# An mLSTM cell and an FP32 feed-forward on one core: products nobody reads from the first microsecond, other buffers for the second chunk's values, and a new order of the front

## The chip, the cores and the metric

The kernel runs on one core of a Trainium2 chip. The core has TensorE (PE, matrix products, with a weight load PEld that overlaps them), VectorE (DVE), ScalarE (ACT), GpSimd (POOL) and SyncE (SP), whose queue issues the DMAs here. The metric is device microseconds of one execution; a profiled execution is looked at beside it.

## The reference

Two stages follow each other. The first is an mLSTM cell over q, k, v of shape (4 batches, 8 heads, 768 steps, 40), with an input, a forget and an output gate:

```python
for t in range(S):
    m_new = np.maximum(f_gate[:, :, t] + m, i_gate[:, :, t])
    f_stab = np.exp(f_gate[:, :, t] + m - m_new)
    i_stab = np.exp(i_gate[:, :, t] - m_new)
    m = m_new
    C = f_stab * C + i_stab * (v_t outer k_t)
    n = f_stab * n + i_stab * k_t
    h_tilde = C @ q_t
    denom = np.maximum(np.abs(n @ q_t), 1.0)
    y[:, :, t] = sigmoid(o_gate[:, :, t]) * h_tilde / denom
```

The loop's bodies are shortened here to what they compute per batch and head. The second stage takes y as 3072 rows of 320, multiplies by w_in (320 x 2048), applies the exact GELU and multiplies by w_out (2048 x 320). The weights lie in DRAM as pairs of 32-bit words, the high and low halves of an FP64 number: the kernel turns them into FP32 itself.

## The kernel before

**Chunks and batches.** The 768 steps are cut into six chunks of 128 (`NCH`), and each chunk has four batches, so a step of the cell is named by a chunk c and a batch b. For chunk 0 the state is zero. `Cell` holds the steps of one chunk. Each step is one letter: `m` mask, `w` weights (the matrix of decays, exponentials on ACT), `g` output gate (a sigmoid on ACT), `t` turn (PE transposes of k and q, copied by ACT), `s` scores (PE, then multiplied into the weights by DVE), `c` carry (PE products into the state and of the state), `v` values (PE), `y` finish (DVE: gate and denominator), `x` turn_y (PE transposes of y, copied by ACT into the feed-forward's input), `r` split_x. Lower case is chunk 0, capitals are chunk 1; the digit behind a letter is the batch.

**Feed-forward.** The rows of chunk 0 go through plain FP32 products: `A` and `U` are up steps (`up_step`, PE and a GELU on ACT; `A` for batches 0 and 1, `U` for 2 and 3), `F` is one of sixteen down rows (`first_down_steps`). Later chunks use products that are split into parts or summed differently (`up`, `down_steps`); the diff does not touch those.

**Weights.** They come in 26 pieces: ten of w_in, sixteen of w_out. `P` fetches a piece; `K` is `conv_one` of the next piece (three DVE operations, two ACT operations), `J` is `conv_two` (two DVE operations), which then fetches the piece four further on. `Z` is `split_weight`, which makes two parts of a piece of w_in for the next chunk's rows.

**The order is written by hand.** `FRONT` is a string of such words, and `play` (near the end of the file) calls the function of each word in turn. Every engine keeps its instructions in that program order, and so does SP's queue of DMAs. An engine waits at an instruction until what it reads is there and what it overwrites is free; all that stands behind on that engine waits too. One exception is in `play`: up steps that were asked for are issued when the next other word comes, or when two are together (`U U`).

**Words of the front that are not of the cell.** `L` loads q and k of a step, `O` v and the output gate. `E` (`second_gates`) and `N` (`later_gates`) compute the gates of chunk 1 and of chunks 2 to 5 with DVE scans, turn them on PE and store the running maximum in DRAM (`M_d`); `B` (`load_M`) loads it back, broadcast. `D` and `Q` (`decays_turned`) turn decay factors: PE transposes, DVE copies, one PE product with `last`. `H` (`products_begin`) opens the pool of later tiles.

**Unread products.** `I` (`keep_clock`) leaves a count in `idle`; the next step that opens a PSUM bank first does that many products of `ident` with itself into it (`unread`), which the real products then overwrite. A later `I` replaces an earlier count that was not used:

```python
def unread(bank):
    for _ in range(idle[0]):
        nc.tensor.matmul(bank, ident, ident, start=True, stop=True, skip_group_check=True)
    idle[0] = 0
```

In the order before, 1 such product stands ahead of w0, 3 ahead of v1, 5 ahead of c1, 2 ahead of s2 and 7 ahead of c2.

**Buffers.** PSUM has the pools `ps_tr` (tag "tr"), `ps_h` (tag "h") and `ps_mm` (tags "a" and "b"), with two buffers for each tag. `carry` and `values` of chunks 0 and 1 take turns in `ps_h`; in chunk 0 the bank of `values` is read by `finish`. From chunk 1 on, `carry` writes what the state gives to a tile `far` (L489), to which `values` adds its part (L527), and which `finish` reads. `far` lies in a pool of two (tag "hs"). The output rows leave through `o_sb`, two buffers of 128 x 2 x 320.

Of the kernel before, what the change touches and what calls it, by code (L numbers as in the profile page):

```python
# [9 lines left out]
F32 = mybir.dt.float32  # L10
# [6 lines left out]
P = 128  # L17
# [8 lines left out]


FRONT = """
    O0 L0 I1 I1 g0 E L1 P0 O2 P1 w0 t0 N D K w1 L2 P2 Q P3 s0 O1 t1 w2 L3 c0 J K v0 K s1 y0 w3 t2 I3 g1 v1 O3 I2 I3
    I5 J c1 B5 I2 K y1 I4 I2 s2 x0 O4 L4 t3 J x1 B4 s3 v2 I7 g3 L5 g2 c2 c3 y2 v3 x2 O5 L6 K J G0 A y3 x3 J H M0 M1  # L30
    K K J T0 W0 O6 M2 O7 A J W1 S0 C0 K J T1 L7 U U K K V0 T2 A M3 J J G1 S1 K W2 W3 K C1 A S2 V1 G2 J Y0 J K
    C2 T3 J K Y1 U U J S3 V2 C3 K J K K J J F K F F F J K J X0 K K J F R0 F F J F K G3 Y2 F J K V3 J K F K X1 J
    J R1 F F F F K X2 B8 J R2 F Y3 Z Z X3 R3 B9 B10 F"""
DOWN = """
    M0 Z M1 W0 F L3 F W1 Z Z F S0 Z S1 K2 C0 M2 Z C1 G0 G1 G2 G3 V0 Z V1 W2 Z M3 F Q2 K3 Q3 Y0 D3 F F W3 F Z S2 S3
    C2 C3 V2 V3 F N F Y1 X0 R0 Y2 F F Y3 X1 R1 F X2 R2 F X3 R3 F"""
# [3 lines left out]
def kernel(  # L40
# [16 lines left out]
    nc = tc.nc  # L57

    B, H, S, D = q.shape
    L = P  # L60
    NCH = S // L
    NP = H // 2
    D1 = D + 1
    DP = 64
    BH = B * H
    DM = H * D
# [15 lines left out]
    two = ctx.enter_context(tc.tile_pool(name="two", bufs=2))  # L82
    outp = ctx.enter_context(tc.tile_pool(name="outp", bufs=2))
    dram = ctx.enter_context(tc.tile_pool(name="dram", bufs=1, space=bass.MemoryType.DRAM))
    ps_tr = ctx.enter_context(tc.tile_pool(name="ps_tr", bufs=2, space=bass.MemoryType.PSUM))
    ps_h = ctx.enter_context(tc.tile_pool(name="ps_h", bufs=2, space=bass.MemoryType.PSUM))
# [9 lines left out]
    w_out = const.tile([P, NF, DM], F32, name="w_out")  # L96
# [32 lines left out]
    def load(n, first=0, end=4):  # L129

        if n >= NCH * B:
            return
        c, b = divmod(n, B)
        for src, dst in ((q, qb), (k, kb), (v, vb), (o_gate, None))[first:end]:
            nc.sync.dma_start(out=dst[turn_of(n)][:, :, 0:D] if dst else out_of(n),
                              in_=src[b, :, c * L:(c + 1) * L, :].rearrange("h p d -> p h d"))
# [13 lines left out]
    def turn_of(n):  # L150

        return n % NLD if n < 2 * B else (n - 2 * B) % NQ
# [38 lines left out]
    for j in range(3):  # L191
        m = slice(BH * j, BH * (j + 1))
        nc.scalar.copy(out=row[m], in_=ident[m, m])
    nc.vector.memset(e_hi, 1151.0 * I23)
    nc.vector.memset(e_lo, 255.0 * I23)

# [5 lines left out]
    def gates_turned(*parts):  # L202

        for src, dst in parts:
            n = dst.shape[1]
            pg = ps_tr.tile([P, n, BH], F32, name="pg", tag="tr")
            for c in range(n):
                nc.tensor.transpose(pg[:, c, :], src[:, c, :], ident[0:BH, 0:BH])
            nc.vector.tensor_copy(out=dst, in_=pg)
# [24 lines left out]
    def decays_turned(e0, e1, g0, g1):  # L234
        e, g = slice(e0, e1), slice(g0, g1)
        gates_turned((ew[:, e], ewT[:, e]), (gg[:, g], gT[:, g]))
        pd = ps_tr.tile([P, g1 - g0, BH], F32, name="pd", tag="tr")
        nc.tensor.matmul(pd.rearrange("p c n -> p (c n)"), last, gT[:, g].rearrange("p c n -> p (c n)"),
                         start=True, stop=True)
        nc.vector.tensor_copy(out=dec[:, g], in_=pd)  # L240
# [4 lines left out]
    for j in range(3):  # L245
        part = M_parts[BH * j:BH * (j + 1)]
        nc.vector.tensor_copy(out=part, in_=left)
        if j < 2:
            nc.vector.tensor_tensor(out=M_left[:, j], in0=left, in1=part, op=OP.subtract)
            left = M_left[:, j]  # L250
    gates_turned((a[:, 0:1], aT[:, 0:1]))

    def second_gates():
        gates_of(1, 2)
        nc.sync.dma_start(out=M_d[0], in_=M[:, 1])
        gates_turned((a[:, 1:2], aT[:, 1:2]))
        decays_of(0, 2, 0, 1)
# [65 lines left out]
    def conv_two(i):  # L323

        if i < len(pieces):
            hi, p = bits.pop(i)[:, :, 1], pow2.pop(i)
            pu = p.bitcast(U32)
            nc.vector.scalar_tensor_tensor(out=pu, in0=hi, scalar=0x80000000, in1=pu,
                                           op0=OP.bitwise_and, op1=OP.bitwise_or)
            dst, s = pieces[i][1], sig.pop(i)  # L330
            nc.vector.scalar_tensor_tensor(out=dst, in0=s, scalar=2.0 ** -20, in1=p, op0=OP.mult, op1=OP.mult)
            fetch(i + NB)
# [10 lines left out]
# [5 lines that stand above are left out]
    def per_head(t, c, b):  # L348
        return t[:, c, b * H:(b + 1) * H].unsqueeze(2)

    class Cell:
# [112 lines left out]
        def carry(self, b):  # L464

            c, n = self.c, self.c * B + b
            qT = self.qT.pop(b)

            pf = ps_h.tile([P, H + NP, D1], F32, name="pf", tag="h")
            pc = pf[:, H:H + NP, :]  # L470
            unread(pf.rearrange("p h d -> p (h d)")[:, 0:P])
            if c == 0:
                self.weigh_values(b)
            if c + 1 < NCH:
                vw = self.vw.pop(b)
                for p in range(NP):
                    for hip in range(2):
                        nc.tensor.matmul(pc[halves[hip], p, :], kb[turn_of(n)][:, 2 * p + hip, :], vw[:, 2 * p + hip, :],  # L478
                                         start=True, stop=True)
            if c > 0:  # L480
                for p in range(NP):
                    for r in halves:
                        nc.tensor.matmul(pf[r, 2 * p:2 * p + 2, :].rearrange("p h d -> p (h d)"), qT[:, p, r],  # L483
                                         state[b][:, p, :], start=True, stop=True)
                if c > 1 and b == B - 1:
                    self.far[b] = qb[2].rearrange("p h d -> p (h d)")[:, 0:H * D1].rearrange("p (h d) -> p h d", d=D1)
                else:
                    self.far[b] = fars[0].tile([P, H, D1], F32, name="far", tag="hs", bufs=2)
                nc.vector.tensor_tensor(out=self.far[b], in0=pf[:, 0:H, :],  # L489
                                        in1=per_head(gT, c - 1, b).to_broadcast([P, H, D1]), op=OP.mult)  # L490
            if c + 1 < NCH:
                for hip in range(2):
                    r, m = halves[hip], slice(D1 * hip, D1 * hip + D1)
                    st = state[b][r, :, m]
                    if c == 0:
                        nc.scalar.copy(out=st, in_=pc[r])
                    else:
                        d = dec[r, c - 1, b * H:(b + 1) * H].rearrange("p (m two) -> p m two", two=2)[:, :, hip:hip + 1]
                        self.engine.tensor_tensor(out=st, in0=st, in1=d.to_broadcast([DP, NP, D1]), op=OP.mult)
                        nc.vector.tensor_tensor(out=st, in0=st, in1=pc[r], op=OP.add)  # L500

            self.read(b)
# [170 lines left out]
    def first_up_steps(h):  # L673

        def step(k):
            ups.append((len(ups) + len(tags_next) % 2, (2 * k, 2 * k + 2, HT * h, HT * h + HT)))
            if len(ups) == 2:
                first_up()

        return [lambda k=k: step(k) for k in range(HF // 2)]  # L680
# [78 lines left out]
    def first_down_steps(g):  # L759
        po = []  # L760

        def row(f):

            if f == 0:
                po.extend(ps_mm.tile([P, DM], F32, name="po", tag="ab"[b // 2]) for b in range(B))
            for b in range(B):
                nc.tensor.matmul(po[b], g.t[:, f, b * L:(b + 1) * L], w_out[:, f, :], start=(f == 0),  # L767
                                 stop=(f == NF - 1))
                if f == NF - 1:
                    if b % 2 == 0:  # L770
                        o_sb = outp.tile([P, 2, DM], F32, name="o_sb", tag="o_sb")
                    nc.scalar.copy(out=o_sb[:, b % 2, :], in_=po[b])
                    send(0, b, o_sb[:, b % 2, :])

        return [lambda f=f: row(f) for f in range(NF)]
# [75 lines left out]
    def in_turn(steps):  # L851
        todo = list(steps)
        return lambda: todo.pop(0)() if todo else None

    def cell_steps(c, letters, before=None):
# [6 lines left out]
    first_g = Hidden(False)  # L862
    n_pieces = range(len(pieces))
    steps = dict(P=fetch, L=lambda n: load(n, 0, 2), O=lambda n: load(n, 2, 4), B=load_M, E=second_gates, N=later_gates,
                 I=keep_clock, D=lambda: decays_turned(0, 2, 0, 1), Q=lambda: decays_turned(2, NCH - 1, 1, NCH - 1),
                 A=in_turn(first_up_steps(0)), U=in_turn(first_up_steps(1)), F=in_turn(first_down_steps(first_g)),
                 K=in_turn(lambda i=i: conv_one(i) for i in n_pieces), H=products_begin,
                 J=in_turn(lambda i=i: conv_two(i) for i in n_pieces), Z=split_weight)
# [42 lines left out]
```

## Time and profile before

The median of three runs is 490.48 us (489.78 to 490.59).

| Quantity | Value |
|---|---|
| The profiled execution's own time | 490.47 us |
| Its span, first to last instruction | 488.7 us |
| Mean granted PE clock | 0.990 |
| PE busy | 472.6 us, 97% of the span |
| DVE busy | 348.0 us, 71% |
| ACT busy | 222.8 us, 46% |
| POOL busy | 69.7 us, 14% |
| Start of the first up step (A) | 44.43 us |
| Start of the first down row (F) | 97.03 us |
| Start of chunk 1's up products | 135.14 us |

Each time in a profile is counted from the start of the span. "Busy" of PE is modelled from pipelined products, so two records can overlap. An FP32 product that is not a transpose shows as two records. A bracket behind an instruction tells how long its engine was idle before it and what ended the idle time.

### The profile page before, as it was taken

How to read it: one execution, taken by the hardware profiler on the slowest of the kernel's cores; microseconds unless marked ns; L12 is line 12 of the kernel's file. 1: busy time of each engine (PE TensorE's matmuls, PEld its weight loads, DVE VectorE, ACT ScalarE, POOL GpSimd, SP SyncE). 2: the span in 40 equal slices, each digit the busy share in tenths (PEclk: the TensorE clock that was granted, in tenths of full speed). 3: DMA queues.
4: the chain of work that ended last, by engine and by line, in shares of the span. 5: the costliest groups of instructions: out<-in, count | busy, mean ns of one | idle time of the engine just before them, and what ended most of it. 6: DMA issues, size and time to landing. Idle time of an engine off the chain costs nothing.

```text
span 488.7 us, 10729 instructions
## 1 busy us (share of the span) xinstructions
PE 472.6 (97%) x4184; PEld 412.8 (84%) x4184; DVE 348.0 (71%) x727; ACT 222.8 (46%) x477; POOL 69.7 (14%) x108
## 2 busy tenths in 40 slices
PE   3899999999999999999999999999999999999997
PEld 3687888877677899987899987899977899977996
DVE  7689787989889998857387757388857388724321
ACT  7595999845444662103762203762203762211300
POOL 3002120000010036200126200126100112000000
PEclk9599999999999999999999999999999999999999
DMA  6979954337561247831256921255931250100001
GB/s 117 236 187 197 239 128 96 107 107 170 102 166 15 27 75 123 166 94 19 31 90 104 200 62 16 34 89 102 190 73 20 32 91 2 36 20 1 1 0 55
DMA packets 164434, 44.24 MB, mean 91 GB/s; under 512 B 154176, under 2 KB 157408, under 8 KB 164384
## 3 DMA queue, kind: packets, MB, share of 16 engines
q1 hardware_dynamic: 164384, 43.56, 45.2%
q8 instruction: 33, 0.54, 0.5%
q14 instruction: 17, 0.14, 0.1%
HBM read 39.52 MB, written 4.01 MB: 89 GB/s over the span
## 4 chain that ended last, share of the span: by engine, by line
PE 88%; ACT 5%; DVE 4%; issue 1%; DMA 0%; SPq 0%; DVEq 0%; ACTq 0%
PE po L790 32%; PE pu L714 21%; PE po L767 7%; PE pu L725 6%; PE pu L659 5%; PE ps L459 4%; PE ph L519 4%; PE pf L483 2%; PE pf L478 2%; PE px L554 1%; PE pu L665 1%; ACT W L390 1%; ACT g L729 1%; PE pt L433 1%; ACT pow L316 1%
## 5 line engine op out<-in xcount | busy, mean ns | idle before, releaser
L790 PE MATMUL po<-w_out,g 128*128 128x160 f32 x640 | 91.2, 300 | 0.0
L729 ACT ACTIVATE g<-pu 128x512 f32<-128x512 f32 x80 | 40.8, 614 | 108.2 <-PE pu L725 108.0
L790 PEld LDWEIGHTS po<-w_out,g 128*128 128x128 f32 x640 | 87.8, 190 | 1.8 <-ACT g L729 1.8
L390 ACT ACTIVATE W<-W,aT 128x128 f32<-128x128 f32 x160 | 48.8, 389 | 3.2 <-POOL W L364 3.1
L790 PE MATMUL po<-w_sums,sums 128*128 128x160 f32 x320 | 47.2, 302 | 0.0
L790 PEld LDWEIGHTS po<-w_sums,sums 128*128 128x128 f32 x320 | 44.2, 190 | 0.4
L564 ACT ACTIVATE x_hi<-px 128x384 fp32r<-128x384 f32 x20 | 9.8, 490 | 73.0 <-PE px L554 73.0
L462 DVE TENSOR_TENSOR W<-ps,W 128x512 f32<-128x512 f32 x48 | 30.2, 684 | 17.4 <-ACT W L390 11.9
L714 PE MATMUL pu<-x_hi,w_in_hi 128*128 128x512 f32 x160 | 41.4, 400 | 0.0
L714 PE MATMUL pu<-x_lo,w_in_lo 128*128 128x512 f32 x160 | 40.6, 396 | 0.0
L364 POOL TENSOR_SCALAR_AFFINE_SELECT W<-W 128x1024 f32<-128x1024 f32 x20 | 23.1, 1162 | 102.8 <-DMA W<-M_d 102.5
L646 DVE TENSOR_TENSOR sums<-g 128x512 f32<-128x512 f32 x20 | 13.8, 690 | 33.3 <-ACT g L729 33.3
L714 PEld LDWEIGHTS pu<-x_hi,w_in_hi 128*128 128x128 f32 x160 | 29.4, 188 | 8.2 <-ACT g L729 1.9
L714 PEld LDWEIGHTS pu<-x_lo,w_in_lo 128*128 128x128 f32 x160 | 30.1, 188 | 7.2
L767 PE MATMUL po<-w_out,g 128*128 128x320 f32 x128 | 35.7, 434 | 0.0
L803 DVE TENSOR_TENSOR o_sb<-po,o_sb 128x320 f32<-128x320 f32 (+1 forms) x27 | 12.5, 465 | 28.7 <-PE po L790 24.9
L714 PE MATMUL pu<-x_all,w_in_mid 128*128 128x512 f32 x80 | 31.7, 396 | 0.1
L767 PEld LDWEIGHTS po<-w_out,g 128*128 128x128 f32 x128 | 23.8, 190 | 9.3
L714 PE MATMUL pu<-x_all,w_mid 128*128 128x512 f32 x80 | 31.7, 396 | 0.0
L618 DVE TENSOR_TENSOR w_in_mid<-w_in_hi,w_in_lo 128x512 fp32r<-128x512 f32 x20 | 14.7, 733 | 21.6 <-PE pu L714 21.6
L659 PE MATMUL pu<-first_x,w_in 128*128 128x256 f32 x128 | 28.8, 381 | 0.5 <-DVE W L462 0.5
L402 POOL MEMSET g<- 32x1024 f32 x8 | 7.6, 945 | 145.0 <-ACT W L390 144.8
(166 smaller groups left out, 882.3 us busy)
## 6 DMA issues: line engine op xcount, KB each, us to landing
W<-M_d SPq DMA_DIRECT2D x20, 512.0 KB, 5.0
bits<-in_moe_w_in_dram SPq DMA_DIRECT2D x20, 256.0 KB, 4.7
bits<-in_moe_w_out_dram SPq DMA_DIRECT2D x16, 320.0 KB, 3.2
ob<-in_o_gate_dram SPq DMA_DIRECT2D x24, 160.0 KB, 3.7
out_dram<-o_sb SPq DMA_DIRECT2D x24, 160.0 KB, 2.4
vb<-in_v_dram SPq DMA_DIRECT2D x22, 160.0 KB, 5.4
kb<-in_k_dram SPq DMA_DIRECT2D x22, 160.0 KB, 4.9
blocks<-in_k_dram SPq DMA_DIRECT2D x48, 32.0 KB, 2.2
```

Source lines behind the costliest of these rows:

```text
L364: nc.gpsimd.affine_select(out=t, in_=t, compare_op=OP.is_ge, fill=1.0e30, base=0, pattern=[[0, H], [1, L]], channel_multiplier=-1)
L390: nc.scalar.activation(out=W[n][:, h, :], in_=src, func=AF.Exp, scale=-1.0, bias=aT[:, self.c, r:r + 1])
L459: nc.tensor.matmul(ps[hip][:, p, :], kT[r, p, :], qT[r, p, :], start=True, stop=True)
L462: nc.vector.tensor_tensor(out=w, in0=ps[hip], in1=w, op=OP.mult)
L519: nc.tensor.matmul(ph[r, h, :], Pm[:, h, r], vb[turn_of(n)][:, h, :], start=True, stop=True)
L618: nc.vector.tensor_tensor(out=w_mid[i], in0=w_hi[i], in1=w_lo[i], op=OP.add)
L659: nc.tensor.matmul(banks[-1][e][:, i - i0, :], in_tile(i, x)[:, e, i % 2 * P:(i % 2 + 1) * P], first_x[:, x, t0:t1], start=(x == 0 and i = ...
L714: nc.tensor.matmul(pus[i][e], w[k][:, e, i * P:(i + 1) * P], x[:, k, :], start=(n == 0 and k == 0), stop=False, skip_group_check=True)
L725: nc.tensor.matmul(pu[e], w[r, i // 2, i % 2 * P:(i % 2 + 1) * P], x[r, NX, :], start=False, stop=(n == 2), skip_group_check=True)
L729: nc.scalar.activation(out=g.t[:, HF * e + i, :], in_=pu[e], func=AF.Gelu, scale=4097.0)
L767: nc.tensor.matmul(po[b], g.t[:, f, b * L:(b + 1) * L], w_out[:, f, :], start=(f == 0), stop=(f == NF - 1))
L790: nc.tensor.matmul(bank[at][:, i, :], lhs(j, t), rhs(j), start=(first and i == 0 and j == 0), stop=(i == n - 1 and j == HF - 1), skip_grou ...
```

## The change

The change has three parts.

- A new function `warm(n)` issues n FP32 products of 128 x 128 with 128 columns into a PSUM tile of `ps_h` that nothing reads. Their operands are a corner of `w_out`, set to 0.5 by a DVE memset at the start. Six stand ahead of all other PE work, six behind the first turned gates, and the new word `k` places further ones: `k3` at the front's start, `k5` and `k1` on both sides of `N`.
- In chunk 1 the tile `far` is now cut from the output buffers (tag "o_sb"), four tiles in turn in two buffers. Chunks 2 to 5 stay as they are.
- `FRONT` has a new order. Of what moves: `P0` and `P1` stand ahead of `L1`, `L3` ahead of `L2`, `O1` behind both; `w1` stands ahead of the first `K`, and that `K` ahead of `Q` and `D`; the counts ahead of unread products are now 2 (w0), 1 (s1), 3 (w3), 6 (v1), 2 (c1), 3 (s2) and none at c2; `v3` stands ahead of `c3`, and `T0` ahead of `c3` and the first `A`; `W0` stands ahead of the second `A`; `T2` ahead of `V0`; `V3` follows `X0` at once; two `F` stand between `X2` and `X3`; one `Z` is early, and `Y3` stands ahead of `R2`.

```diff
 FRONT = """
-    O0 L0 I1 I1 g0 E L1 P0 O2 P1 w0 t0 N D K w1 L2 P2 Q P3 s0 O1 t1 w2 L3 c0 J K v0 K s1 y0 w3 t2 I3 g1 v1 O3 I2 I3
-    I5 J c1 B5 I2 K y1 I4 I2 s2 x0 O4 L4 t3 J x1 B4 s3 v2 I7 g3 L5 g2 c2 c3 y2 v3 x2 O5 L6 K J G0 A y3 x3 J H M0 M1
-    K K J T0 W0 O6 M2 O7 A J W1 S0 C0 K J T1 L7 U U K K V0 T2 A M3 J J G1 S1 K W2 W3 K C1 A S2 V1 G2 J Y0 J K
-    C2 T3 J K Y1 U U J S3 V2 C3 K J K K J J F K F F F J K J X0 K K J F R0 F F J F K G3 Y2 F J K V3 J K F K X1 J
-    J R1 F F F F K X2 B8 J R2 F Y3 Z Z X3 R3 B9 B10 F"""
+    k3 O0 L0 g0 I2 I2 E P0 w0 t0 P1 L1 k5 N k1 O2 P2 L3 L2 w1 K Q D s0 O1 t1 w2 c0 P3 K v0 I1 J K s1 y0 I4 I3 w3 t2
+    I6 O3 v1 g1 L4 J I2 c1 I2 I3 K y1 s2 x0 t3 O4 B5 x1 J L5 B4 s3 v2 g3 g2 c2 v3 y2 T0 H G0 c3 K J x2 O6 y3 O5 A x3
+    J M1 K K J M0 W0 L6 A J M2 W1 S0 C0 T1 K J U U K K T2 V0 A O7 J W2 G1 K M3 J K S1 C1 G2 Y0 L7 A W3 S2 V1 J J Y1
+    C2 K T3 J K U U J S3 V2 K C3 K J K J J F K F F J F K X0 J G3 K J K V3 F F F J R0 K Y2 Z J F K K F J F K X1 J F R1
+    F J K F X2 F B8 F Y3 J Z X3 R2 B9 R3 B10 F"""
...
+    def warm(n):
+        cold = ps_h.tile([P, P], F32, name="cold", tag="h")
+        for _ in range(n):
+            nc.tensor.matmul(cold, w_out[:, 0, 0:P], w_out[:, 0, 0:P], start=True, stop=True, skip_group_check=True)
+
+    nc.vector.memset(w_out[:, 0, 0:P], 0.5)
+    warm(6)
     nc.vector.memset(e_hi, 1151.0 * I23)
...
     gates_turned((a[:, 0:1], aT[:, 0:1]))
+    warm(6)
...
-                if c > 1 and b == B - 1:
+                if c == 1:
+                    self.far[b] = outp.tile([P, 2, DM], F32, name="far", tag="o_sb").rearrange("p two d -> p (two d)")[:, 0:H * D1].rearrange(
+                        "p (h d) -> p h d", d=D1)
+                elif b == B - 1:
                     self.far[b] = qb[2].rearrange("p h d -> p (h d)")[:, 0:H * D1].rearrange("p (h d) -> p h d", d=D1)
...
-                 I=keep_clock, D=lambda: decays_turned(0, 2, 0, 1), Q=lambda: decays_turned(2, NCH - 1, 1, NCH - 1),
+                 I=keep_clock, k=warm, D=lambda: decays_turned(0, 2, 0, 1), Q=lambda: decays_turned(2, NCH - 1, 1, NCH - 1),
```

## The prediction

> **What bounds the kernel now.** I read the page's forty slices first:
>
> ```profile
> PE   3899999999999999999999999999999999999997
> DVE  7689787989889998857387757388857388724321
> ACT  7595999845444662103762203762203762211300
> PEclk9599999999999999999999999999999999999999
> ```
>
> TensorE (PE) is full from the third slice (12.2 us a slice) to the end. The diff touches only steps before 135 us; later work can only be moved. What can be won is there: idle PE, unread products, half clock. The table of stretches places the half clock:
>
> ```profile
> 12.50:15.00 2.50, 0.95 (x5) 0.73 (x6) 2.01 (x7) 1.15 (x2) 0.00 (x0) 0.92 1.19 242
> 15.00:17.50 2.50, 2.50 (x18) 1.71 (x18) 1.62 (x5) 1.63 (x4) 0.00 (x0) 0.50 1.05 282
> 22.50:25.00 2.50, 2.50 (x24) 1.64 (x23) 2.43 (x6) 1.96 (x7) 0.00 (x0) 0.53 1.13 209
> 25.00:30.00 5.00, 5.00 (x90) 4.51 (x87) 4.34 (x11) 4.88 (x13) 0.00 (x0) 1.00 0.92 197
> ```
>
> (busy us of PE, its weight loads, DVE, ACT, POOL; then clock, DMA share, GB/s). The clock is half from about 14.3 to 24.5 us. The 1.00 recorded earlier is only partly true: groups by form from 9.4-10.0 and 11.2-11.7 show the same transpose at two speeds, so the clock came up near 10.9:
>
> ```profile
> L433 PE MATMUL pt<-ident,kb 128*128 128x128 f32 x1 | 0.4, 421 | 0.0
> L433 PE MATMUL pt<-ident,blocks 128*128 128x128 f32 x3 | 0.6, 317 | 0.0
> ```
>
> Next the chain in order of time (start, length), cut to the front:
>
> ```profile
> 13.71 0.60 DVE gg L229
> 18.21 0.79 PE pd L238 x2
> 19.00 2.01 PE ps L459 x16
> 21.01 1.90 PE pt L433 x8
> 23.80 1.61 ACT W L390 x6
> 34.75 0.73 ACT pow L316
> 39.98 1.76 PE pf L345 x14
> 44.70 3.46 PE pu L659 x16
> ```
>
> DVE's gates carry it to 14.3, PE at half clock to 23.8, ACT without a gap to 37.7, PE from there. In the timeline, two PE waits remain after 44 us:
>
> ```profile
> 58.71 1.99 PE L659 MATMUL pu<-first_x,w_in 128*128 128x256 f32 x8 [0.52 <-DVE W L462]
> 132.86 0.41 PE L554 MATMUL px<-ident,ob 128*128 128x128 f32 x2 [1.02 <-DVE ob L537]
> ```
>
> **What the Trainium skill says.** "TensorE: Matmul & The Clock Gate", Part 1 (the HAM clock gate): half clock is the default; a busy free-running window of about 3.4 us raises it, an idle one drops it. The trace agrees: changes near 10.9, 14.3 and 24.5 lie one and three windows apart. The window 10.9-14.3, some 1.4 us of work, dropped it; 34.7-38.1, with 2.3, kept it; 17.7-21.1, with 2.8, did not raise it. The same page, Part 4, says transposes don't count as busy in the same way; no row here separates that. "FP8 and Floating Point Precision", TensorE Precision Notes: true FP32 takes four passes. An unread product shows as two records; fourteen records take 1.76 us, so 0.25 us for one at full clock. At half clock I take 0.5; two records alone took 0.80 with their tails and 0.59 to the next instruction, so 0.4 to 0.59.
>
> **The change, part by part.** Sums stand against the profiled execution: span 488.7, 1.77 around it, 490.47 in all; the median is 490.48.
>
> *First products.* One DVE memset of 128x128 (POOL's alike takes 0.20) hides in DVE's 1.04 us wait for f_sb. Six products run from about 1.0 to 4.0, where today's first transpose stands at 3.96; six more and k3 follow, 9 x 0.5 = 4.5 us to 8.8 at half clock. A full window falls in 1.0-7.8 whatever its phase, so the clock rises between 4.4 and 7.8, and they end between 6.6 and 8.3. E's transpose, due at 7.38, is queued behind them, DVE's copy to aT (7.94) behind that and N's gates behind the copy: 0 to 0.7 us late, I take 0.2. With k5 the next PE work is t0's transposes (ready near 9.6) plus 1.25, ending near 11.7; N's transposes wait until 12.0 for ACT's kT copy anyway: nothing. k1 (0.25) lies ahead of w1, whose ACT work waits for 14.98: nothing.
>
> *w1 ahead of K, K ahead of Q and D.* N's last DVE result ends at 14.31, its ACT step at 14.98. w1's exponentials then run 14.98-17.1, the pair of conv_one to 18.5; ACT then idles, as today, so this gives nothing. K's DVE part, 1.45 us (0.42 + 0.42 + 0.69), now precedes Q's copies: 15.8, copies 0.23 + 0.29, sums on PE 0.4, then D's copies and sum with their hand-overs, about 1.9 us: s0 starts near 18.3, today 18.93. Gain 0.6.
>
> *The clock then.* From 13.6 to 18.2 PE holds only Q and D, some 1.9 us of small work in 4.6. For six phases in ten a window in it holds under 1.4 us, as the one that dropped the clock. I take that it drops. Then s0 (2.01) and t1 (1.90) stay slow, t1's copies come near 21.4 (today 22.09), w2's exponentials at 23.1 (23.80): gain 0.7.
>
> *ACT's run.* From w2 to g1 ACT goes 23.80-34.24 without a pause: w2 2.02, states 0.63, two conv_one 1.39 + 1.47, w3 2.02, t2 1.14, table load 1.30, gate 0.47. The new order has the same steps, so g1 ends at 33.5. y1, s2, t3, x1 and s3 follow at the same distances: s3's DVE product starts at 38.3, today 38.95. Gain 0.6. Unread products I1, I3, I6, I2, I3 (3.75 us) lie under ACT's run.
>
> *After s3.* The seven unread products at c2 (1.76) go, but c2 waits for vw2 (to 40.0), and v3 now precedes c3 with y2's three reads of the bank between: v3 at 40.9, T0 (0.87, moved ahead of the first A) 41.95-42.8, c3, x2, first A at 43.8. Today A starts at 44.43 and T0 follows: gain 0.6 + 0.87 on PE. T0's two ACT copies (53.36-54.43, 1.07) leave the stretch between the first Gelu and W0 that released the second pair at 58.71. So U U starts at 58.71 - 0.7 - 1.07, about 56.9, PE being ready at 56.4. Gain 1.8. W0 now lies ahead of the second Gelu on ACT; that bank is wanted only 3.5 us into U U, as now.
>
> *DMAs.* On SP, P0 and P1 go ahead of L1, L3 ahead of L2, O1 after them, L4 and B5 earlier. By bytes at 210 GB/s (estimate from the table), P0 lands near 12 (due 14.3), L1 near 15-17 (due 20), L2 24 (due 28), P3 28 (due 31), B4 46.5 (W0 due 52). M_d's two stores wait for DVE as now and hold the queue. Nothing, with 2 us of cover.
>
> *Far values.* They move to the two output buffers, which the last F fills on ACT; far[3] is read by Y3 some 2 us earlier. Nothing; up to 0.5 if Y3 is late.
>
> *Last rows.* Two F (4.35 us) instead of one stand between X2 and X3, and Y3 precedes R2. The 1.02 wait goes. DVE must do Y3 and the last J before the last F: 29.2 us of work from S3's product plus 3.5 us of waits for pow, as now, ends J at 130.0, F needs it at 130.4. V3 after four F instead of nine needs S3's product, 8 us old. The early Z hides in the same sum.
>
> Sum: 1.8 + 1.0 - 0.2 = 2.6. **Forecast 490.47 - 2.6 = 487.9.**
>
> **Rivals.**
> (B) *The clock holds through 13.6-18.2.* s0 and t1 then take half: 2.0 more, all ahead of ACT's run: 485.7. For: phase, and an unknown threshold. Against: the window 10.9-14.3.
> (C) *DVE becomes the bound in the last rows.* DVE is 4.0-4.8 of 5 busy there; if each K is followed at once by its own J, twelve waits of 0.46 instead of about six add 2.7, less the 0.4 of cover: the X3 gain and more go, 489.8 at the end and 489.2 in the middle.
> (D) *It doesn't do what it says.* The clock never comes up by k5. The products then hold PE: t0 ends at 13.0, k5 at 15.5, N's transposes delay DVE by 2.4, s0 comes 2 late; T0 and X3 give back 1.9: 490.4. Against: the continuous stretch that raised the clock at 10.9.
> (E) *The clock falls a second time, slower.* Without c2's products PE is loosely filled from 34 to 42; a window below what 34.7-38.1 held (2.3 of 3.4 us) drops it, and s3, v2, c2, v3, T0, c3 (5.2 us, most of them on the chain) run twice as long until a full window: + 4.2, 492.1. It turns to slower once over 3.6 us of chain work lie under half clock. For: my timetable leaves 2.35 in the window from 36.2. Against: as much was enough before.
>
> **How the numbers follow.** Forecast 0.42 (own range 487.0 to 489.0), B 0.18, C 0.10, D 0.13, E 0.17. A difference under 0.2%, 1 us, is about what a measurement here can't tell from none. Faster takes the forecast, B and most of C: 0.68; same D and the rest: 0.15; slower E: 0.17. The range 485.3 to 490.9 leaves out E and the tails.
>
> **What would show it.** The unread products from 1 us and a transpose at 317 ns before 9 us; clock 0.5 again between 16 and 19 (right) or not (B); s0's first score near 18.3; w2's exponentials at 23.1; first pu at 43.8; the second pair at 56.9; no wait ahead of the last px; the last J just ahead of the last F. Wrong would be: aT late by over 0.7, a DVE wait on a late load, or half clock after 30 us.

## The result, and the profile after

The changed kernel takes 488.52 us (median of eight runs, 488.05 to 488.96) where the kernel before, run beside it, takes 489.75 (eight runs, 489.48 to 490.59). The ratio is 0.9971 (95% interval 0.9961 to 0.9982), faster by 1.4 us; the two medians lie 1.2 us apart. The profiled execution took 488.88 us for a span of 487.1; before, 490.47 for 488.7. So the profiles differ by 1.6 us.

The forty slices of the changed kernel:

```profile
PE   8898999999999999999999999999999999999997
DVE  7689888888979997857398857397767397724321
ACT  7596999954434862203861203862203861211300
PEclk9799999999999999999999999999999999999999
```

PE's first slice went from 3 to 8: the unread products. The clock's low slice is still there (7 after, 5 before). The stretches of the changed kernel (us, then busy us of PE, its weight loads, DVE, ACT, POOL; clock, DMA share, GB/s) show when:

```profile
12.50:15.00 2.50, 1.22 (x13) 0.65 (x10) 2.46 (x7) 1.17 (x3) 0.00 (x0) 1.00 1.21 228
15.00:17.50 2.50, 1.75 (x9) 1.28 (x9) 1.53 (x5) 2.50 (x9) 0.00 (x0) 0.70 0.95 161
22.50:25.00 2.50, 2.50 (x58) 2.08 (x56) 2.43 (x5) 2.42 (x9) 0.00 (x0) 0.94 1.16 170
```

The clock falls at 16.0 us, after a stretch in which PE had little to do, and is back at 22.8. The same reading in finer stretches gives 14.6 and 24.9 for the kernel before. The chain of the changed kernel in order of time (start, length), cut to the pieces that answer to those shown of before:

```profile
17.91 0.63 PE pd L246 x2
18.55 2.01 PE ps L468 x16
20.56 1.90 PE pt L442 x8
23.16 1.06 ACT W L399 x4
33.12 0.47 ACT ob L405
38.32 1.09 DVE W L471 x2
40.95 1.19 DVE ob L549
44.49 3.46 PE pu L671 x16
```

Scores and transposes still last 2.01 and 1.90 us, so they still run at half clock, but all is 0.2 to 0.6 us earlier (before, scores from 19.00, exponentials from 23.80, products from 44.70). Four lines of the changed kernel's timeline, among them the two that answer to the waits of before:

```profile
7.38 0.25 PE L216 MATMUL pg<-ident,a 32*128 32x32 f32 x1 [0.19 <-DVE a L224]
57.55 2.64 PE L671 MATMUL pu<-first_x,w_in 128*128 128x256 f32 x11 [0.43 <-DVE W L471]
130.71 0.38 PE L566 MATMUL px<-ident,ob 128*128 128x128 f32 x2
132.95 2.23 PE L726 MATMUL pu<-x_hi,w_in_hi 128*128 128x512 f32 x8
```

The second pair starts at 57.55 (58.71 before), the last `px` of chunk 0 has lost its wait of 1.02 us, and chunk 1's up products start at 132.95 (135.14 before). That is 2.19 us earlier, but only 1.6 arrive at the end. The chain shows where 0.5 goes, in the cell of chunk 2:

```profile
178.72 4.34 DMA W<-M_d
185.81 1.02 DVE ob L549
187.59 1.88 DVE W L471 x3
189.52 1.02 PE ph L531 x28
```

A load of the running maximum, which stands behind block loads on SP's queue, was issued at 178.72, 1.25 us earlier than before, while PE's work was 2.2 us earlier. The same load in the profile of before:

```profile
179.97 0.38 SPq L160 DMA_DIRECT2D W<-M_d  x1
```

Masks, values and scores follow it, and PE's `ph` has to wait for DVE. So from chunk 1's up products to chunk 2's it takes 74.05 us where the kernel before takes 73.54.

### The profile page after: what moved, and what is told of

Same layout as the page of the kernel before. It is cut to its first block, busy times and chain, and to the rows that moved or that the text cites. A ratio compares the mean times of both kernels' runs of the same rounds, so it can differ in the third digit from the quotient of the medians.

```text
span 487.1 us, 10810 instructions
## 1 busy us (share of the span) xinstructions
PE 477.2 (98%) x4224; PEld 417.9 (86%) x4224; DVE 345.8 (71%) x728; ACT 222.5 (46%) x477; POOL 69.3 (14%) x108
## 3 DMA queue, kind: packets, MB, share of 16 engines
q1 hardware_dynamic: 164384, 43.56, 45.3%
## 4 chain that ended last, share of the span: by engine, by line
PE 84%; DVE 6%; ACT 5%; DMA 1%; issue 1%; POOL 1%; SPq 1%; DVEq 0%; POOLq 0%
PE po L802 30%; PE pu L726 21%; PE po L779 7%; PE pu L737 6%; PE pu L671 5%; PE ps L468 4%; PE ph L531 3%; PE pf L492 2%; PE px L566 1%; PE pu L677 1%; PE pf L487 1%; ACT W L399 1%; DMA W<-M_d 1%; ACT g L741 1%; PE pt L442 1%
## 5 line engine op out<-in xcount | busy, mean ns | idle before, releaser
L373 POOL TENSOR_SCALAR_AFFINE_SELECT W<-W 128x1024 f32<-128x1024 f32 x20 | 22.1, 1109 | 97.9 <-DMA W<-M_d 85.3
L815 DVE TENSOR_TENSOR o_sb<-po,o_sb 128x320 f32<-128x320 f32 (+1 forms) x27 | 12.5, 463 | 28.0 <-PE po L802 24.1
```

The source lines that it names most:

```text
L373: nc.gpsimd.affine_select(out=t, in_=t, compare_op=OP.is_ge, fill=1.0e30, base=0, pattern=[[0, H], [1, L]], channel_multiplier=-1)
```

## The experiments

My theory before them: the time comes from the last rows (about 1.0) and from the front (about 1.6, through s0, ACT's run and the first A); the first products themselves give nothing; the half clock that is left is worth some 2 us more. The rivals: the first products are what helps; the front is bound by ACT or DVE, so that clock is worth nothing; each small part (order of `T0`, of `B5`, c2's seven products, the far tiles) has its own price. All ratios are to the kernel before, run beside; a ratio is not simply that of two medians, and the kernel before's own median went from 489.75 to 490.45 us between the series, so kernels are compared by their ratios.

**e1: without the first products.** The changed kernel less the memset, both sixes and all `k`.

```diff
-    k3 O0 L0 g0 I2 I2 E P0 w0 t0 P1 L1 k5 N k1 O2 P2 L3 L2 w1 K Q D s0 O1 t1 w2 c0 P3 K v0 I1 J K s1 y0 I4 I3 w3 t2
+    O0 L0 g0 I2 I2 E P0 w0 t0 P1 L1 N O2 P2 L3 L2 w1 K Q D s0 O1 t1 w2 c0 P3 K v0 I1 J K s1 y0 I4 I3 w3 t2
...
-    nc.vector.memset(w_out[:, 0, 0:P], 0.5)
-    warm(6)
...
-    warm(6)
```

> The changed kernel without its new products: no memset of w_out's corner, none of the two sixes, no k3, k5, k1. Theory: they give nothing, because up to 14.3 us DVE's gates set the pace and the clock falls again near 16 us. Then w2's exponentials start at 23.0 to 23.5 (changed kernel 23.16, before 23.80) and the time stays within 0.4 us of the changed kernel's (ratio to before 0.9962 to 0.9980). Rival: the products are what brings s0 and w2 forward. Then w2 falls back to 23.8 or later and the ratio rises to 0.9985 or more.

Measured: 0.9970 (0.9958 to 0.9981), 488.52 us, the changed kernel's own median. So in the time the first products give nothing that can be told (the intervals leave some 0.6 us either way). A stretch and s0's scores in its profile:

```profile
17.50:20.00 2.50, 2.22 (x15) 2.02 (x17) 0.56 (x3) 0.94 (x2) 0.00 (x0) 1.00 0.97 227
```

```profile
18.61 2.08 PE L465 MATMUL ps<-qT,kT 64*128 64x128 f32 x16
```

The column says clock 1.00, but sixteen scores take 2.08 us: ahead of the trace's first entry for the clock the column shows 1.00, whatever the clock is. Here that entry, a full clock, stands at 24.1 us; in the changed kernel's trace it stands at 5.7. So the clock was at half until 24.1 us, and s0 was still only 0.13 us later than with the products.

**e2: the last rows alone.** The kernel before, with the new end of `FRONT`.

```diff
-    J R1 F F F F K X2 B8 J R2 F Y3 Z Z X3 R3 B9 B10 F"""
+    J R1 F F F K X2 F B8 F Y3 J Z Z X3 R2 B9 R3 B10 F"""
```

> The kernel before with the end of its front alone in the new order: two F instead of one between X2 and X3, Y3 and the last J ahead of R2. Theory: the 1.02 us wait ahead of the last px goes and nothing takes its place: minus 1.0 us, ratio 0.9979, chunk 1's up products at 134.1 instead of 135.1. Rival: DVE is the bound there, and the last J comes too late for the last F: ratio 0.999 to 1.001, with a PE wait ahead of the last po rows or of the first pu rows.

Measured: 0.9976 (0.9969 to 0.9983), 489.15 us. So the last rows alone give 1.2 us, most of what the whole change gives (1.4). From the first F to chunk 1's up products it takes 36.90 us where the kernel before takes 38.11. The surprise is its front, which is the old order. Three stretches and four lines of its profile:

```profile
15.20:18.60 3.40, 3.02 (x18) 1.92 (x15) 1.99 (x7) 2.96 (x9) 0.00 (x0) 0.50 1.08 250
18.60:22.00 3.40, 3.40 (x23) 3.18 (x24) 1.62 (x4) 0.92 (x4) 0.00 (x0) 0.50 1.03 193
22.00:24.00 2.00, 2.00 (x44) 1.60 (x43) 1.97 (x5) 1.89 (x7) 0.00 (x0) 1.00 1.09 238
```

```profile
17.73 0.80 PE L238 MATMUL pd<-gT,last 128*128 128x128 f32 x2 [0.38 <-DVE gT L209]
22.80 2.18 ACT L390 ACTIVATE W<-pm,aT 128x128 f32<-128x128 f32 x8
57.69 2.64 PE L659 MATMUL pu<-first_x,w_in 128*128 128x256 f32 x11 [0.51 <-DVE W L462]
130.66 0.38 PE L554 MATMUL px<-ident,ob 128*128 128x128 f32 x2
```

The same order as before reaches w2's exponentials at 22.80 and the second pair at 57.69, where the profile of before has 23.80 and 58.71. The clock was back at 22.0 instead of 24.9. The fall is at 15.2 in e2's profile and 14.6 in that of before, so the half clock lasts 6.8 us in one and 10.2 in the other. Cut at 3.4 us from the fall on, the profile of before reads:

```profile
11.20:14.60 3.40, 1.37 (x11) 0.80 (x10) 3.19 (x10) 2.02 (x6) 0.00 (x0) 1.00 1.17 258
14.60:18.00 3.40, 3.22 (x19) 2.29 (x19) 1.95 (x6) 2.51 (x7) 0.00 (x0) 0.50 1.06 254
18.00:21.40 3.40, 3.19 (x20) 2.75 (x21) 0.73 (x3) 1.37 (x6) 0.00 (x0) 0.50 1.09 206
21.40:24.80 3.40, 3.40 (x24) 2.54 (x22) 3.37 (x7) 2.17 (x6) 0.00 (x0) 0.50 1.12 220
```

```profile
18.21 0.79 PE L238 MATMUL pd<-gT,last 128*128 128x128 f32 x2 [0.38 <-DVE gT L209]
```

In both profiles the clock comes back at the end of the first such stretch that PE fills. The one wait of 0.38 us ahead of `pd` lies across the edge at 18.0 in the profile of before, so that neither stretch beside it is full; in e2's it lies within the first, and the second is full. This is read from the profiles; no run moved the wait alone.

The executions timed say the same. Each lists its mean granted clock. Of the 27 of the kernel before that ran beside e1 to e4, ten have 0.991 to 0.993 and took 489.46 to 490.06 us (median 489.62). The other seventeen, with 0.989 to 0.990 or 0.999 to 1.000, took 490.15 to 491.33 (median 490.53). e2 splits alike: seven at 488.32, fifteen at 489.30 (medians). The old front thus has two lengths, 0.9 to 1.0 us apart, and the profile that the prediction was summed against is one of the long ones (clock 0.990). A mean of 1.000 need not be a full clock, as e1's profile shows: half clock ahead of the first entry isn't counted.

**e3: the clock held.** The changed kernel, with seven more unread products between w1 and s0: three ahead of `K`, three inside `Q` and one inside `D` (the expectations of e3, e7 and e9 count eight; the trace has 14 records more than the changed kernel's, two to a product).

```diff
-    ... P2 L3 L2 w1 K Q D s0 ...
+    ... P2 L3 L2 w1 k3 K Q D s0 ...
...
-    def gates_turned(*parts):
+    def gates_turned(*parts, fill=(0, 0)):
...
-        for src, dst in parts:
+        for (src, dst), more in zip(parts, fill):
...
+            if more:
+                warm(more)
...
-                 I=keep_clock, k=warm, D=lambda: decays_turned(0, 2, 0, 1), Q=lambda: decays_turned(2, NCH - 1, 1, NCH - 1),
+                 I=keep_clock, k=warm, D=lambda: decays_turned(0, 2, 0, 1, (0, 1)), Q=lambda: decays_turned(2, NCH - 1, 1, NCH - 1, (1, 2)),
```

> The changed kernel with eight more unread products where PE stands idle between 13.4 and 18.2 us: three ahead of Q, one and two inside Q, one inside D. If the fall of the clock near 16 us is what keeps s0 and t1 slow, the clock stays up, s0 takes 1.1 us instead of 2.1 and w2's exponentials start near 21.2; about 2.0 us go: ratio 0.993 (486.5). Rival: the chain is bound by ACT and DVE at that place whatever the clock does, or the clock falls at a later idle stretch: w2 starts earlier, but the first pu stays within 0.5 us of 44.3 and the ratio at 0.996 to 0.998.

Measured: 0.9923 (0.9900 to 0.9946), 485.85 us, by the two ratios 2.4 us less than the changed kernel, and the fastest kernel of this study. Stretches of 3.4 us, first of the changed kernel up to the fall of its clock, then of e3:

```profile
12.60:16.00 3.40, 1.55 (x15) 0.87 (x12) 3.37 (x9) 2.17 (x7) 0.00 (x0) 1.00 1.11 195
```

```profile
13.60:17.00 3.40, 2.93 (x21) 2.11 (x19) 2.78 (x9) 3.17 (x11) 0.00 (x0) 1.00 1.32 179
34.20:37.60 3.40, 2.44 (x53) 2.08 (x52) 2.87 (x6) 1.42 (x4) 0.00 (x0) 1.00 1.09 253
```

And e3's timeline:

```profile
17.87 1.16 PE L470 MATMUL ps<-qT,kT 64*128 64x128 f32 x16
20.62 2.19 ACT L401 ACTIVATE W<-pm,aT 128x128 f32<-128x128 f32 x8
54.51 1.35 PE L673 MATMUL pu<-first_x,w_in 128*128 128x256 f32 x5 [0.43 <-DVE W L473]
```

With 2.93 of 3.4 us filled, where the changed kernel has 1.55 just ahead of the fall, the clock stays, s0's scores take 1.16 us instead of 2.08, w2 comes 2.54 us earlier and the second pair 3.04. The rival that ACT or DVE would bind falls. One of its six executions took 489.33 us; its clock is 0.993, the others' 0.999 to 1.000. By these clocks it was not held in that one.

**e4: `B5` later.** In the changed kernel's profile y2's last product on DVE lay under a POOL mask:

```profile
40.70 1.09 POOL L373 TENSOR_SCALAR_AFFINE_SELECT W<-W 128x1024 f32<-128x1024 f32 x1 [35.41 <-DMA W<-M_d]
40.95 1.18 DVE L549 TENSOR_TENSOR ob<-ob,den 128x320 f32<-128x320 f32 x1
```

The same product takes 0.49 us in the profile of before. The mask waits for the load that `B5` issues, so e4 moves `B5` behind `L5`.

```diff
-    ... t3 O4 B5 x1 J L5 B4 s3 ...
+    ... t3 O4 x1 J L5 B5 B4 s3 ...
```

> The changed kernel with B5 moved behind L5 on SP's queue, so that POOL's mask of that tile no longer falls into y2. Theory: in the changed kernel this mask (POOL, 40.70 to 41.79) stretched y2's last product on DVE from 0.49 to 1.18 us and so held vw3, c3 and the first pu, 0.6 us later than forecast. Then that product takes 0.49 again, the first pu starts at 43.7 instead of 44.3, and the second pair at about 56.9 instead of 57.55: minus 0.6 us, ratio 0.9958. Rival: the stretch of y2 is met again at another DVE operation, or the pair waits for W0 on ACT whatever A does: ratio 0.9966 to 0.9976.

Measured: 0.9970 (0.9958 to 0.9982), 488.34 us: not told apart from the changed kernel, so the 0.6 us of my expectation don't show in the time. In its profile the mask and the product no longer meet:

```profile
41.28 0.49 DVE L549 TENSOR_TENSOR ob<-ob,den 128x320 f32<-128x320 f32 x1
45.51 1.09 POOL L373 TENSOR_SCALAR_AFFINE_SELECT W<-W 128x1024 f32<-128x1024 f32 x1 [40.23 <-DMA W<-M_d]
```

The first `pu` then starts 5.54 us after s3's product on DVE, against 6.03 in the changed kernel, and the second pair 18.76 us after it, against 19.25. The collision is worth 0.5 us of this stretch in a profile. But s3's product itself comes 15.52 us behind w2's exponentials (15.14 in the changed kernel; cause not settled), and the pair starts at 57.40, only 0.15 us earlier. The collision can fall on another product too: in e5's profile the mask meets one a little later on DVE, which takes 1.38 us instead of 0.49, and the second pair comes 19.45 us after s3's product.

**e5: the new order with the old last rows.**

```diff
-    F J K F X2 F B8 F Y3 J Z X3 R2 B9 R3 B10 F"""
+    F J K F F X2 B8 J R2 F Y3 Z X3 R3 B9 B10 F"""
```

> The changed kernel with the old end of the front: one F between X2 and X3, R2 and the last J ahead of Y3; all else of the change stays. If the end alone gives the gain (it gave a ratio of 0.9976 by itself, against 0.9971 for the whole change), the ratio is 0.9990 to 1.0005 and the 1.0 us wait ahead of the last px is back. If the rest of the front gives the 1.6 us that the prediction put down to it, the ratio is 0.9965 to 0.9985 here.

Measured: 0.9996 (0.9988 to 1.0004), 490.04 us. The wait is back:

```profile
131.49 0.41 PE L566 MATMUL px<-ident,ob 128*128 128x128 f32 x2 [1.02 <-DVE ob L549]
```

Everything but the last rows is worth 0.2 us, give or take 0.4. Twenty of its 21 executions have a clock of 0.991 to 0.993, with a median of 489.96; the ten of the kernel before with that clock, run beside, have 489.53, the other nineteen 490.47. So against the old front's short form the new kernel is some 0.4 us slower, against its long form 0.5 faster. Its profile has one candidate for the 0.4: chunk 2's cell loses 0.5 us there, as in the changed kernel (74.05 us). The clock is not all: the twenty executions with 0.991 to 0.993 go from 489.20 to 491.49 us. A loss behind the front that differs from one execution to the next would do that, but only one of them was profiled.

**e6: `T0` behind x3**, as it was before.

```diff
-    ... c2 v3 y2 T0 H G0 c3 K J x2 O6 y3 O5 A x3
-    J M1 ...
+    ... c2 v3 y2 H G0 c3 K J x2 O6 y3 O5 A x3
+    T0 J M1 ...
```

> The changed kernel with T0 behind x3 again, as in the order before. Prediction's step: T0's two ACT copies (1.07 us) then stand ahead of W0 again and T0 on PE (0.87) behind the first A, so the first pu comes 0.5 to 0.9 us earlier (43.5), but the second pair 1.0 later (58.6 instead of 57.55): ratio 0.9991. Rival: the earlier first A makes up for it, and the pair stays within 0.3 us of 57.55: ratio 0.9968 to 0.9978.

Measured: 0.9961 (0.9948 to 0.9973), 488.27 us: not slower than the changed kernel. ACT from the first Gelu on, the changed kernel ahead, then e6:

```profile
49.05 1.09 ACT L681 ACTIVATE g<-pu 128x512 f32<-128x512 f32 x2 [1.03 <-PE pu L677]
54.56 2.45 ACT L399 ACTIVATE W<-W,aT 128x128 f32<-128x128 f32 x8
```

```profile
47.70 1.09 ACT L681 ACTIVATE g<-pu 128x512 f32<-128x512 f32 x2 [1.03 <-PE pu L677]
49.03 0.62 ACT L445 COPY kT<-pt 128x512 f32<-128x512 f32 x1
49.50 0.63 ACT L445 COPY qT<-pt 128x512 f32<-128x512 f32 x1
54.18 2.45 ACT L399 ACTIVATE W<-W,aT 128x128 f32<-128x128 f32 x8
```

With `T0` behind, its two copies are back between the Gelu and W0 and cost 0.95 us there, but the first A, and with it the Gelu, comes 1.35 us earlier: `T0` no longer stands ahead of it, in this profile the mask does not hold DVE up, and s3's product is 0.24 us earlier. From s3's product to the first `pu` it takes 4.92 us, where e4, whose mask is away too, takes 5.54: `T0` ahead of the first A costs 0.62 us, on PE by its transposes (`c3` follows them without a wait in e4). `T0` also has a product on DVE, a `vw` that stands ahead of `c3`'s; in the changed kernel's profile, with the mask on top, `c3` waits 0.42 us for DVE. The second pair starts 19.11 us after s3's product here and 18.76 in e4, so `T0`'s new place is worth 0.35 us of the 0.97 that leave ACT, and the time doesn't show it. What saves the copies makes A late.

**e7: the clock held, without the first products.** e3, less both sixes, `k3` at the start, `k5` and `k1` (the memset stays, as the held products read it).

```diff
-    k3 O0 L0 g0 I2 I2 E P0 w0 t0 P1 L1 k5 N k1 O2 P2 L3 L2 w1 k3 K Q D s0 ...
+    O0 L0 g0 I2 I2 E P0 w0 t0 P1 L1 N O2 P2 L3 L2 w1 k3 K Q D s0 ...
...
-    warm(6)
...
-    warm(6)
```

> The kernel with eight products in the idle places of 13.4 to 18.2 us, but without the two sixes, k3, k5 and k1. If what counts is only that PE is full in some window ahead of s0, the clock is up by 18 us all the same: s0 takes 1.1 us, w2 starts at 20.6 to 21.2, ratio 0.9920 to 0.9945. If the clock has to be up already, by the products of the first 12 us, so that the later ones only keep it, s0 takes 2.1 us, w2 starts at 22.5 or later, ratio 0.9960 or more.

Measured: 0.9939 (0.9916 to 0.9961), 487.35 us. In its profile s0's scores start at 17.86 and take 1.16 us, as in e3: the first products are not needed for that. Its profiled execution loses 0.9 us in chunk 2's rows, where e3's loses nothing (table below): `px` waits for a copy on DVE that takes 1.11 us instead of 0.22, while a product and the masks run on POOL.

```profile
199.15 1.11 DVE L555 COPY y_rest<-ob 128x128 f32<-128x128 f32 x1
```

One of its six executions took 485.32 us, four 487.14 to 487.50, one 489.92. By the two ratios e3 is 0.8 us faster, but the intervals overlap; whether the first products earn any of it stays open, the more so as this loss lies far behind the front.

**e8: the clock held in the old order.** The kernel before with the first products, and seven more inside `D` and `Q`.

```diff
-    O0 L0 I1 I1 g0 E L1 P0 O2 P1 w0 t0 N D K w1 ...
+    k3 O0 L0 I1 I1 g0 E L1 P0 O2 P1 w0 t0 k5 N D K w1 ...
...
+    nc.vector.memset(w_out[:, 0, 0:P], 0.5)
+    warm(6)
...
-                 I=keep_clock, D=lambda: decays_turned(0, 2, 0, 1), Q=lambda: decays_turned(2, NCH - 1, 1, NCH - 1),
+                 I=keep_clock, k=warm, D=lambda: decays_turned(0, 2, 0, 1, (2, 4)), Q=lambda: decays_turned(2, NCH - 1, 1, NCH - 1, (0, 1)),
```

> The kernel before, in its old order throughout, with the change's first products (two sixes, k3, k5) and seven more in the idle places inside D and Q. If the half clock from 14.3 to 24.5 us is on the path in the old order too, s0 starts near 17.5 and takes 1.1 us, w2's exponentials start near 20.5 instead of 23.80 and 2 to 3 us go: ratio 0.9940 to 0.9960. Rival: the old order puts w1's exponentials behind the first conv_one, so ACT or DVE holds w2 at 22.5 or later: ratio 0.9975 or more.

Measured: 0.9956 (0.9941 to 0.9971), 487.52 us (six of eight executions at 487.39 to 488.52, two near 489.5). The half clock lay on the path in the old order too. Its w2 starts at 20.21, earlier than e3's 20.62, so the new order isn't what brings s0 and w2 forward. The wait in its last rows is there, 1.02 us, as in the kernel before.

**e9: e3 with `T0` behind x3.** The edit is e6's, on e3.

> Two parts together: the eight products that held the clock (ratio 0.9923) and T0 behind x3 again (0.9961 for the changed kernel with that alone). If the two add up, the first pu starts at 40.0, the second pair near 54.3, and the ratio is 0.9905 to 0.9925. If the first A, once it is earlier, lowers what PE has to do between 34 and 42 us so far that the clock falls there, s3 to A take longer and the ratio is 0.995 or more.

Measured: 0.9938 (0.9914 to 0.9962), 486.03 us, not told apart from e3. The first `pu` came at 40.68 instead of 41.29, the second pair at 55.14 instead of 54.51. So in these two profiles `T0`'s new place is worth 0.63 us at the second pair; e6 had the smaller ratio with `T0` behind, e9 has the larger, and in both pairs the intervals overlap: the times don't settle it. One of the seven executions took 489.97 us at a clock of 0.993; there, as in one of e3's, the clock was not held.

**e10: e8 with the new last rows.** The edit is e2's, on e8.

> The kernel before with two things only: the products that hold the clock (0.9956 alone) and the new end of the front (0.9976 alone). If the rest of the new order gives nothing, this is as fast as the changed kernel with a held clock: ratio 0.9915 to 0.9940, and 0.9932 if the two add up. If the rest of the order has its 1.6 us once the clock is equal, this stays 1.2 us or more behind that kernel's 0.9923: ratio 0.9948 or more.

Measured: 0.9950 (0.9931 to 0.9968), 488.26 us (486.52 to 488.92), where e8 with the gain of e2 would give about 486.3 and only the fastest executions come near. The last rows do lose their wait. DVE in e8, then in e10, in the stretch behind w2:

```profile
23.32 0.43 DVE L324 TENSOR_SCALAR pow<-bits 128x512 uint32<-128x512 uint32 x1 [0.16 <-DMA bits<-in_moe_w_in_dram]
```

```profile
24.53 0.43 DVE L324 TENSOR_SCALAR pow<-bits 128x512 uint32<-128x512 uint32 x1 [1.37 <-DMA bits<-in_moe_w_in_dram]
```

In the old order, once the clock holds, DVE waits here for a piece of w_in, 0.16 us in one profile and 1.37 in the other; chunk 2's cell loses another 1.2 us in e10's. In its profile both together are what e10 lacks. In the profiles of e3, e7 and e9, which have the new order of the loads, DVE has no such wait between 16 and 50 us. That points to a use of that order: it has cover for an earlier front, which the change itself doesn't reach. No run shows it alone.

**e11: the far values back in their own tiles.**

```diff
-                if c == 1:
-                    self.far[b] = outp.tile([P, 2, DM], F32, name="far", tag="o_sb").rearrange("p two d -> p (two d)")[:, 0:H * D1].rearrange(
-                        "p (h d) -> p h d", d=D1)
-                elif b == B - 1:
+                if c > 1 and b == B - 1:
```

> The changed kernel with chunk 1's far tiles in the pool of two (tag hs) again, as before the change. Nothing waits for either pool in the profiles, so the ratio stays that of the changed kernel (0.9971) within 0.001. Rival: the output buffers hold up the last F or the first rows of the next stage, and taking far out of them gives 0.3 us or more: ratio 0.996 or less.

Measured: 0.9962 (0.9950 to 0.9973), 488.33 us: the far tiles' place is worth nothing that can be told.

**e12: seven unread products at c2 again.**

```diff
-    ... B4 s3 v2 g3 g2 c2 v3 y2 T0 ...
+    ... B4 s3 v2 I7 g3 g2 c2 v3 y2 T0 ...
```

> The changed kernel with the seven unread products ahead of c2 again. PE stands idle 0.72 us there and the products take 1.75, so c2, v3, T0, c3 and the first pu come 1.0 us later (45.3 instead of 44.3). By the chain from the first Gelu to W0 the second pair comes 1.0 later too: ratio 0.9991. Rival: c3 waits for DVE's two products with vw anyway, so A moves by 0.3 us at most: ratio 0.997 to 0.998.

Measured: 0.9967 (0.9954 to 0.9980), 488.82 us. The first `pu` starts 6.25 us after s3's product, 0.2 later than in the changed kernel; from w2 to the second pair it is 34.60 (34.39). But in e12's profile the mask comes too late to hold `vw` or `c3`, so e4 is the one to set it against: there the first `pu` comes 5.54 us and the pair 18.76 us after s3's product, here 6.25 and 19.47. The seven products cost 0.7 us of the 1.0 expected in that profile; in the time, with 0.6 us of interval either way, they don't show.

**All profiles side by side** (us; the last column is from chunk 1's up products to chunk 2's):

| Kernel | First F | Chunk 1's up | Chunk 2's cell and rows |
|---|---|---|---|
| before | 97.03 | 135.14 | 73.54 |
| changed | 96.06 | 132.95 | 74.05 |
| e1 | 96.56 | 133.45 | 73.54 |
| e2 | 96.00 | 132.90 | 73.53 |
| e3 | 93.02 | 129.91 | 73.55 |
| e4 | 95.90 | 132.80 | 73.54 |
| e5 | 95.65 | 133.75 | 74.05 |
| e6 | 95.68 | 132.58 | 73.52 |
| e7 | 93.66 | 130.55 | 74.49 |
| e8 | 93.62 | 131.73 | 73.53 |
| e9 | 93.65 | 130.54 | 73.55 |
| e10 | 94.62 | 131.52 | 74.74 |
| e11 | 96.37 | 133.27 | 73.52 |
| e12 | 95.41 | 132.30 | 73.62 |

From the first F to chunk 1's up products it is 38.10 or 38.11 us in the three kernels with the old last rows (before, e5, e8) and 36.89 or 36.90 in the eleven with the new ones: 1.21 us, whatever the front and the clock.

Four of fourteen lose 0.5 to 1.2 us behind the front, with and without the new order. In three (changed, e5, e10) it goes at the `ph` of chunk 2's cell, and there the load is issued 45.3 to 46.1 us after chunk 1's up products, against 43.9 to 45.4 in the others; e7 loses it later, by DVE and POOL, as shown. What makes the load late in the three was not settled; a kernel with the same front can be without it (e4, e6).

## Why the prediction was right, and where not

The sign and the time were right: 488.52 for a forecast of 487.9, inside both ranges. The gain was half of the 2.6 us forecast, 1.2 by the medians and 1.4 by the ratio; that the time came so near is in part luck, as the kernel before took 489.75 beside it and not the 490.47 that the sum starts from. The mechanism was right for the last rows and for the clock, and wrong for what the new front earns.

- *First products.* They came as said: 0.94 us of them end just before E's transpose, which starts at 7.38, so nothing is late (0.2 was taken). The clock's first entry stands at 5.7 us (4.4 to 7.8 forecast). e1 shows nothing of them in the time.
- *w1 ahead of K, K ahead of Q and D; the clock then.* s0 at 18.48 (18.3 forecast), clock down at 16 and slow through s0 and t1, w2 at 23.16 (23.1). Each number is met, and yet the step fails: it credits 0.7 us to the order. e2 has the old order, with s0 at 18.46 and w2 at 22.80. What the profile of before had against it was a clock that came back at 24.9 instead of 22.0. One profile of before was taken for the kernel, and that the numbers are met is luck: in the six profiles of the new order with the first products and no held clock w2 starts at 22.30 to 23.16. The six phases in ten for the fall were too few: in all six of these profiles the clock fell, after stretches with 1.4 to 2.1 us of PE work in 3.4. The entries for the clock of before stand at 11.2, 14.6 and 24.9, 0.3 to 0.4 us later than was read from its groups and stretches.
- *ACT's run.* As forecast: gate done at 33.59 (33.5), s3's product at 38.30 (38.3). It follows from the start of w2, so its 0.6 us rest on the same step.
- *After s3.* From s3's product to the second pair 1.16 us less was forecast (18.6 for 19.76). The profile has 0.51 (19.25), and e4, where DVE doesn't meet POOL's mask, 1.00 (18.76). So the term was mis-sized by the mask: the sum moved `B5` and gave it no price, and A (its weight load) started at 44.22 instead of 43.8. That `T0`'s copies leave the stretch is right (0.97 less between the first Gelu and W0's table load, 1.07 forecast); set against e4, e6 shows that `T0` takes 0.62 of it back on PE. The seven products at c2 are worth 0.7 in a profile (e12). Another 0.2 us goes on the way to the first F (38.51 us from the second pair, before 38.32); its cause is open.
- *DMAs and far values.* Nothing, as forecast (no load was late in the front; e11).
- *Last rows.* Right: 1.0 forecast, 1.2 measured by e2 alone and 1.21 between all profiles with and without them, and their undoing in e5 takes the gain away. DVE ended the last J at 130.14 (130.0 forecast) ahead of an F at 131.04, so rival C didn't come.
- *Later work can only be moved.* So the first part of the prediction had it, and it failed in the changed kernel's profile: 0.5 of the 2.19 us won by chunk 1 was lost in chunk 2's cell, where a load did not move as far as PE's work.
- *Sum.* Of 2.6 the last rows hold. The front's share, 1.8 less 0.2, is 0.2 in the time, give or take 0.4 (e5). In the profiles it looked like more because the profile of before has a late clock. What the change does to the clock is to make its record repeatable: seven of eight executions of the changed kernel have 0.992 to 0.993, twenty of e5's 21 0.991 to 0.993, but only 24 of 67 of the kernel before have 0.991 to 0.993. e1, without the first products, has 1.000 in three of six, and its profile shows the late rise behind such a value; so I put this down to the first products, without having shown it.

Of the rivals, B was the one with substance. The clock did fall, as the forecast had it, but holding it would have been worth 2.2 us by B's sum; e3 gives 2.4, and e8 shows it in the old order. E, a second fall between 34 and 42 us, was not seen in any of the fourteen profiles: 2.44 us of 3.4 kept the clock in e3, close to the 2.3 that the prediction had from before. D was half seen: without the first products the clock may not come up (e1), at no cost in the median that can be told.

## What to carry to other kernels

Where a short front hangs on the PE clock, profile it several times before summing against it: two executions of one order can differ by more than the edit is worth, and the granted clock that each execution lists helps to tell them apart, with the trap that 1.000 can stand for a clock that held and for one that came up late. Unread products pay where a window would otherwise run empty just ahead of PE work on the critical path, not where PE merely waits at the start; seven of them in the right 4 us, added to the change, gave 2.4 us where the whole change gave 1.4, though the clock was lost all the same in one of six executions (e3) and one of seven (e9). A step moved ahead of another to clear one engine's stretch must be priced on the engine where it now stands in the way.

## What the runs showed of the hardware

- The moment at which the clock rises or falls differs between executions of the same instructions: down at 14.6 and back at 24.9 us in the profile of before, 15.2 and 22.0 in e2's, for the same front; it is worth 0.9 to 1.0 us. The traces' entries for the clock lie 3.41, 6.83 or 10.24 us apart in the eight profiles that have a fall ahead of 25 us, one, two and three times 3.41. The Trainium skill, "TensorE: Matmul & The Clock Gate", Part 1, says that the window runs freely and that one kernel measures different numbers of cold products by its phase; these runs agree, and give the price here.
- Cut into stretches of 3.41 us from these entries, the traces show what went ahead of a change. In the eight stretches that ended in a fall PE was busy for 1.4 to 2.1 us; the thinnest ones in the fronts that kept the clock have 2.05 (e10) and 2.3 (before). At half clock in these eight profiles, stretches with 2.4 to 3.2 us didn't bring it back, and each that did was full. Busy time of PE is modelled and tells nothing of the kind of work, and 2.05 kept what 2.10 lost (e12), so this is no threshold.
- The clock of a stretch reads 1.00 ahead of the trace's first entry, whatever the clock is: in e1 that entry stands at 24.1 us. Until then only the length of known products (sixteen scores in 1.16 or 2.08 us) tells.
- A POOL mask holds up a DVE product of two SBUF operands that starts after it: 1.18 us for 0.49, ending 0.34 us after the mask does (42.13 and 41.79). Under a mask a DVE copy (1.16 us for 0.23, e11) and an operation with one tensor input (1.31 for 0.42, e12) grew as well. The Trainium skill, "SBUF — State Buffer", section "SBUF: two separate sides", says that the two engines share a port pair that one holds for a whole instruction, for a DVE operation with two SBUF inputs too. The lines shown under e4 agree in the main: behind the mask the product still needs 0.34 us, not its whole 0.49.
